# A fused attention and two-layer feed-forward kernel: the second pair's first scores get PSUM of their own, and two loads and two chunks of work change place

## The chip, the core and the metric

The kernel runs on one core of a Trainium2 chip. The core has five engines with an instruction queue each: TensorE (PE in the profile; its weight loads are PEld), VectorE (DVE), ScalarE (ACT), GpSimd (POOL) and SyncE (SP, which here only issues DMAs). Each queue runs in the order in which the program was written, and engines wait for each other through semaphores. TensorE writes its results into PSUM, 128 partitions of 8 banks; a bank holds 512 fp32 numbers a partition. The metric is the device time of one execution in microseconds (us), as the median of several runs.

## What is computed

With 2 batches, 12 heads, 448 positions and a head size of 64 (cut from the reference):

```
scores = q @ k.T / 8, upper triangle masked with -1e9
attn   = exp(scores - max) ; attn /= sum + 1e-9
x      = (attn @ v) as 896 tokens x 768
xn     = x / sqrt(mean(x*x) + 1e-6) * rms_g
y      = (silu(xn @ w_gate) * (xn @ w_val)) @ w_out      # 768 -> 1536 -> 768
out    = relu(y @ w_in)**2 @ w_out2                      # 768 -> 2048 -> 768
```

All of it is fp32.

## The kernel before

**Pairs.** Attention runs over 12 pairs of heads (two heads of one batch, side by side on the 128 partitions); function `step(p)` writes one pair. Its steps, by the short names used from here on:

- *s1* (lines 362 and 366): masked scores of query rows 0 to 127 (128 keys) and 256 to 383 (384 keys), in two chunks of 128 and 384 columns a head, into one PSUM buffer of 1024 numbers (two banks). *s2* (lines 362 to 378): those of rows 128 to 255 (256 keys) and 384 to 447 (448 keys), into another buffer of that kind.
- maxima on VectorE (lines 408 and 406), their negative on ScalarE (line 413, tile `nb`), exponentials with sums on ScalarE (line 433; four for s1 into `p1`, three for s2 into `p2t`).
- reciprocals of the sums on VectorE (lines 448 and 449; *r1* for s1, *r2* for s2), and the seven scalings by them on GpSimd (line 459).
- *tp* and *tp2*: transposes on TensorE (line 475), two PSUM tiles `t` of one bank for `p1` and two for `p2t`; each is copied to SBUF (`pt`, line 311) by ScalarE or VectorE.
- *o*: probabilities times values on TensorE (lines 508 and 513), one bank; then a copy into a `row` tile, its square (line 538 or 540), and the sum of squares (line 543).

After six pairs the first batch can be normalised (function `norm`, lines 575 to 613), and the first products of the feed-forward part can begin (function `whole_tiles`, matmuls of line 897, into the score buffers). When all pairs are done the second batch is normalised, and the remaining 2097 matmul instructions (line 693) run to the end. Weights are loaded in chunks (`raw`, line 633), unpacked on ScalarE (lines 646 and 641) and VectorE (line 651), and split into a high and a low part (`ring`, lines 268, 270 and 678).

**PSUM.** Two score buffers `s` (four banks), three `t` banks, one `o` bank. With two score buffers, a pair's s1 takes the buffer that held the s1 of the pair before it; it can start when that pair's four exponentials are done.

**Order.** The steps are not written out in their final order. `step` and the others give each step a due time, the engines that may run it with a cost on each, and the steps and buffers that it needs (`add`); `Order.run` is a planner that goes through a modelled time and issues what can go first, choosing an engine where there is a choice. So a change of a buffer or of a due time moves instructions on all engines, and from one engine to another.

**The start.** Twelve matmuls on zeros (`WARM`, line 1065) run while the first loads are under way; `IDLE = (5, 3)` puts five more behind pair 0's s2 and three behind pair 1's s1, into the `o` bank. They compute nothing.

Of the kernel before, what the change touches and what calls it, by code (L numbers as in the profile page):

```python
# [9 lines left out]
F32 = mybir.dt.float32  # L10
# [4 lines left out]
AF = mybir.ActivationFunctionType  # L15
ALU = mybir.AluOpType
PSUM = bass.MemoryType.PSUM

B, H, S, D = 2, 12, 448, 64
DM, DF1, DF2 = 768, 1536, 2048  # L20
P = 128
# [3 lines left out]
NF1 = DF1 // P  # L25
NF2 = DF2 // P
NPAIR = H // 2
WARM = 12
IDLE = (5, 3)
ACC = 0.0  # L30
CN = 112
# [1 line left out]
STRIDE = 5.5  # L33
# [22 lines left out]
class Order:  # L56
# [15 lines left out]
    def add(self, due, opts, f, after=(), new=(), uses=(), mode=None, begin=0.0, prev=(), port=False):  # L72

        t = dict(due=due, opts=opts, f=f, port=port, after=[a for a in after if a], new=list(new), uses=list(uses) + list(new),
                 mode=mode, begin=begin, end=None, eng=None, i=len(self.tasks), prev=[a for a in prev if a])
        for b in t["uses"]:
            b.left += 1
        self.tasks.append(t)  # L80
        return t
# [106 lines left out]
def tile_attention_moe_moe2(ctx: ExitStack, tc: tile.TileContext, qk, v, wg, wv, wo, w2i, w2o, rms_g, out):  # L188
# [12 lines left out]
    nc = tc.nc  # L201
# [5 lines left out]
    psum = ctx.enter_context(tc.tile_pool(name="psum", bufs=1, space=PSUM))  # L207
# [8 lines left out]
                  s=([P, 1024], F32))  # L216
    order = Order(dict(qk=3, v=3, p1=2, p2=2, pt=2))
    add, chain, buf = order.add, order.chain, order.buf
# [3 lines left out]
    def have(pool, **n):  # L222
        for name, k in n.items():
            for _ in range(k):
# [9 lines left out]

                order.more(name, make)

    def banks(name, *which):
        for i in which:
            order.more(name, lambda i=i: psum.tile([P, 512], F32, tag=f"b{i}", name=name, bufs=1))

    have(psum, s=2)
    banks("t", 0, 1, 2)
    banks("o", 3)
    have(pw, raw=2, wt=2, st=4, ring=8)
    have(pt_, snap=5, tt=2, uu=2, part=6, row=14)

# [3 lines left out]
    warm = atc.tile([P, 256], BF16, name="warm")  # L250
# [5 lines left out]
    g_sb = const.tile([P, NCC], F32, name="g_sb")  # L256
# [6 lines left out]
    def E(c):  # L263
        return {"A": nc.scalar, "D": nc.vector, "P": nc.gpsimd}[c]
# [13 lines left out]
    NPR = B * NPAIR  # L278
# [4 lines left out]
    for i, fill in enumerate((1.0, -1.0e9 * float(D) ** 0.5)):  # L283
        for k in range(2):
            for sl in (slice(0, D), slice(D, P)):
                t = half[sl, 2 * i + k]
                nc.gpsimd.affine_select(
                    out=t, in_=t, pattern=[[-1, P]], compare_op=ALU.is_ge if i else ALU.not_equal, fill=fill,
# [6 lines left out]
    for i in range(NV):  # L295
        t = atc.tile([P, 4, 2 * D], F32, name=f"vt{i}")
# [3 lines left out]
    for i in range(2):  # L300
        t = atc.tile([P, 2, 512], F32, name=f"p2t{i}")
# [11 lines left out]
    def A_(n, acc=0):  # L313
        return 0.17 + 0.00085 * n + (0.08 + ACC if acc else 0.0)
# [4 lines left out]
    def P_(n, two=False):  # L319
        return 0.2 + 0.0022 * n if two else 0.22 + 0.0009 * n  # L320
# [10 lines left out]
    def step(p):  # L331

        z = pairs[p]
        T0 = p * STRIDE
        bq, bv, b1, b2, bp1, bp2 = (order.buf(n) for n in ("qk", "v", "s", "s", "p1", "p2"))
        bpt, bo, bx = (order.buf(n) for n in ("pt", "o", "row"))

        def load_qk(e):
# [46 lines left out]


        if p < len(IDLE):
            bi = order.buf("o")

            def zeros(e):  # L390
                for _ in range(IDLE[p]):
                    nc.tensor.matmul(bi.tile[:, :256], warm[:, :P], warm, start=True, stop=True)

            add(T0, {"E": 0.11 * IDLE[p] + 0.16}, zeros, [(t3, t2)[p]], new=[bi], mode="w")
# [42 lines left out]
        ex_ = []  # L437
        for k, (buf, h, o, n, dst) in enumerate((
                ("s1", 0, 0, 128, "p1"), ("s1", 1, 0, 128, "p1"), ("s1", 0, P, 384, "p1"), ("s1", 1, P, 384, "p1"),
                ("s2", 0, 0, 256, "p2"), ("s2", 1, 0, 256, "p2"), ("s2", 0, 256, 448, "p2"))):  # L440
            b, bp = (b1, bp1) if k < 4 else (b2, bp2)
# [4 lines left out]
        def over(a, b):  # L446
            def f(e):
                nc.vector.tensor_scalar(z["r"][:, a:b], z["su"][:, a:b], 1.0e-9, 1.0, ALU.add, ALU.mult)
                nc.vector.reciprocal(z["r"][:, a:b], z["r"][:, a:b])  # L449
            return f  # L450

        r1 = add(T0 + 4, {"D": 0.37}, over(0, 4), ex_[:4], port=True)
        r2 = add(T0 + 7, {"D": 0.37}, over(4, 7), ex_[4:], port=True)

        def ml(k):
            def f(e):
                t = (z["p1"][:, k % 2, 0:128] if k < 2 else z["p1"][:, k % 2, 128:512] if k < 4 else
                     z["p2"][:, 0, (k - 4) * 256:(k - 3) * 256] if k < 6 else z["p2"][:, 1, :S])
                E(e).tensor_scalar(t, t, z["r"][:, k:k + 1], 1.0, ALU.mult, ALU.mult)  # L459
            return f  # L460

        ml_ = []
        for k, n in enumerate((128, 128, 384, 384, 256, 256, 448)):
            ml_.append(add(T0 + (5 if k < 4 else 8), {"P": P_(n)}, ml(k), [r1 if k < 4 else r2],
                           uses=[bp1 if k < 4 else bp2]))


# [57 lines left out]
        b = p // NPAIR  # L525
# [382 lines left out]
        have(p, part=18, row=18)  # L908

    add(0.0, {"X": 0.0}, rows_come, used)  # L910
    norm(0, (NPAIR + 4.5) * STRIDE, 5.0)
    norm(1, 0.0, 0.3)
    ws = []
    for k in range(2 * NE):
        due = 20 + 14.0 * k
        c, t = weights((wg, wv)[k % 2][k // 2], NCC, due, due, "wt")
        ws.append([form((c, o, t), 3, due) for o in (0, 3 * P)])
    whole_tiles(0, ws, 1000.0)
# [139 lines left out]
        f = halved(h2, k, highs(f), m, 2.0)  # L1058
        due = seven(w2o, k, f, of, due, k == 12, m=m)

    add(30.0, {"S": 2.0}, lambda e: nc.sync.dma_start(out=g_sb, in_=rms_g))
    with tc.manual_schedule():
        ps = psum.tile([P, 512], F32, tag="b3", name="warm", bufs=1)
        for _ in range(WARM):
            nc.tensor.matmul(ps[:, :256], warm[:, :P], warm, start=True, stop=True)
        order.run()
# [36 lines left out]
```

## Time and profile before

| | |
|---|---|
| median of 3 runs | 544.83 us (542.96 to 547.33) |
| the profiled execution | 543.9 us, its span 542.1 us |
| TensorE busy | 531.3 us, 98% of the span |
| VectorE, ScalarE, GpSimd busy | 447.8, 407.2, 311.3 us |
| granted TensorE clock | 1.00 through the span |

The span is the time from the first to the last instruction on the profiled core; 1.8 us of the execution's time lie around it. A busy time is the union of an engine's instructions. An arrow in brackets behind a row, as `[1.40 <-ACT p L433]`, is idle time of that engine just before the row, and what ended it. A row with `xN` merges N instructions that follow closely; its start is that of the first.

### The profile page before, as it was taken

How to read it: one execution, taken by the hardware profiler on the slowest of the kernel's cores; microseconds unless marked ns; L12 is line 12 of the kernel's file. 1: busy time of each engine (PE TensorE's matmuls, PEld its weight loads, DVE VectorE, ACT ScalarE, POOL GpSimd, SP SyncE). 2: the span in 40 equal slices, each digit the busy share in tenths (PEclk: the TensorE clock that was granted, in tenths of full speed). 3: DMA queues.
4: the chain of work that ended last, by engine and by line, in shares of the span. 5: the costliest groups of instructions: out<-in, count | busy, mean ns of one | idle time of the engine just before them, and what ended most of it. 6: DMA issues, size and time to landing. Idle time of an engine off the chain costs nothing.

```text
span 542.1 us, 8954 instructions
## 1 busy us (share of the span) xinstructions
PE 531.3 (98%) x3049; PEld 470.5 (87%) x3049; DVE 447.8 (83%) x831; ACT 407.2 (75%) x879; POOL 311.3 (57%) x349
## 2 busy tenths in 40 slices
PE   7999999999999999999999999999999999999997
PEld 5776766898899999999999989999898998899996
DVE  4788868599998887989867877998776799889795
ACT  4989887566867766679888777877878998886730
POOL 4666566215341452258999789242822886789910
PEclk9999999999999999999999999999999999999999
DMA  8255522113153333333544153134333333332333
GB/s 244 88 162 161 161 49 103 50 68 117 60 172 119 118 116 118 121 120 109 180 129 149 66 177 116 60 116 176 117 117 117 117 117 116 118 117 79 85 138 137
DMA packets 19502, 65.07 MB, mean 120 GB/s; under 512 B 2048, under 2 KB 8960, under 8 KB 19456
## 3 DMA queue, kind: packets, MB, share of 16 engines
q1 hardware_dynamic: 19376, 64.27, 36.0%
q8 instruction: 24, 0.39, 0.3%
q10 hardware_dynamic: 80, 0.23, 0.2%
q14 instruction: 22, 0.18, 0.1%
HBM read 61.74 MB, written 2.75 MB: 119 GB/s over the span
## 4 chain that ended last, share of the span: by engine, by line
PE 60%; DVE 18%; ACT 11%; DMA 4%; POOL 4%; issue 4%; DVEq 0%; POOLq 0%; ACTq 0%
PE m L693 45%; DVE ring L678 4%; DVE part L561 4%; PE t L475 4%; PE o L513 3%; PE s L362 3%; DMA raw<-in_w2i 2%; ACT ring L270 2%; PE s L375 2%; POOL part L561 2%; ACT s L641 2%; ACT raw L646 2%; PE s L897 1%; DVE s L651 1%; DVE row L725 1%
## 5 line engine op out<-in xcount | busy, mean ns | idle before, releaser
L693 PE MATMUL m<-part,ring 128*128 128x448 f32 x2097 | 424.4, 364 | 2.8 <-ACT snap L311 1.4
L693 PEld LDWEIGHTS m<-part,ring 128*128 128x128 f32 x2097 | 392.6, 188 | 34.4 <-ACT snap L311 4.4
L561 POOL TENSOR_TENSOR part<-row,part 128x448 fp32r<-128x448 f32 x103 | 122.5, 1210 | 51.1 <-ACT part L270 50.2
L678 DVE TENSOR_TENSOR ring<-s,ring 128x384 fp32r<-128x384 f32 (+1 forms) x159 | 83.1, 537 | 28.7 <-ACT ring L270 28.0
L725 POOL TENSOR_TENSOR row<-row 128x448 f32<-128x448 f32 x64 | 76.7, 1214 | 29.8 <-ACT row L1040 12.0
L270 ACT CAST ring<-s 128x384 fp32r<-128x384 f32 (+1 forms) x159 | 72.1, 470 | 25.7 <-PE m L693 12.9
L270 ACT CAST part<-row 128x448 fp32r<-128x448 f32 x133 | 70.1, 572 | 7.4 <-POOL wt L705 3.3
L646 ACT ACTIVATE raw<-raw 128x768 uint32<-128x768 uint8 (+1 forms) x70 | 62.7, 897 | 10.6 <-DMA raw<-in_w2i 3.7
L641 ACT ACTIVATE s<-raw 128x768 f32<-128x768 f32 (+1 forms) x64 | 53.6, 849 | 9.4 <-DVE ring L678 8.0
L651 DVE SCALAR_TENSOR_TENSOR s<-s,raw 128x768 uint32<-128x768 uint32 (+1 forms) x64 | 48.0, 749 | 6.4 <-ACT s L641 5.4
L268 POOL TENSOR_SCALAR ring<-st 128x384 fp32r<-128x384 f32 (+1 forms) x12 | 6.2, 512 | 79.1 <-DVE st L705 68.2
L270 ACT CAST ring<-st 128x384 fp32r<-128x384 f32 (+1 forms) x52 | 24.7, 504 | 25.3 <-DVE st L705 21.9
L678 POOL TENSOR_TENSOR ring<-st,ring 128x384 fp32r<-128x384 f32 (+1 forms) x39 | 38.0, 989 | 6.7 <-ACT ring L270 5.9
L705 DVE TENSOR_TENSOR s<-s,st 128x384 f32<-128x384 f32 (+1 forms) x62 | 34.2, 551 | 1.7
L561 DVE TENSOR_TENSOR part<-row,part 128x448 fp32r<-128x448 f32 x43 | 32.0, 769 | 2.8 <-ACT part L270 2.6
L408 DVE TENSOR_REDUCE mx<-s 128x2 f32<-128x256 f32 (+2 forms) x36 | 24.0, 687 | 11.2 <-PE s L378 6.3
L705 DVE TENSOR_TENSOR st<-st,s 128x384 f32<-128x384 f32 (+1 forms) x62 | 32.9, 531 | 0.2
L459 POOL TENSOR_SCALAR p<-p,r 128x128 f32<-128x128 f32 (+1 forms) x48 | 23.0, 497 | 16.7 <-DVE r L449 16.2
L311 ACT COPY snap<-m 128x448 f32<-128x448 f32 x51 | 27.1, 531 | 3.8 <-PE m L693 3.8
L459 POOL TENSOR_SCALAR p2t<-p2t,r 128x256 f32<-128x256 f32 (+1 forms) x36 | 22.7, 644 | 9.2 <-DVE r L449 5.3
L362 PE MATMUL s<-qk 64*128 64x128 f32 (+2 forms) x144 | 24.7, 426 | 2.0 <-ACT p L433 1.4
L979 DVE TENSOR_TENSOR row<-m,row 128x448 f32<-128x448 f32 x36 | 22.1, 618 | 3.8 <-PE m L693 3.5
(100 smaller groups left out, 574.3 us busy)
## 6 DMA issues: line engine op xcount, KB each, us to landing
raw<-in_w2i SPq DMA_DIRECT2D x16, 768.0 KB, 4.2
raw<-in_wg SPq DMA_DIRECT2D x12, 768.0 KB, 4.7
raw<-in_wv SPq DMA_DIRECT2D x12, 768.0 KB, 4.3
raw<-in_wo SPq DMA_DIRECT2D x12, 768.0 KB, 4.3
raw<-in_w2o SPq DMA_DIRECT2D x12, 768.0 KB, 4.6
qk<-in_qk SPq DMA_DIRECT2D x11, 448.0 KB, 3.8
raw<-in_w2o SPq DMA_DIRECT2D x6, 512.0 KB, 3.8
out_t<-row SPq DMA_DIRECT2D x12, 224.0 KB, 1.9
```

What stands on the lines that cost most here:

```text
L270: eng.copy(o, i)
L311: (nc.scalar.copy if e == "A" else nc.vector.tensor_copy)(o, i)
L362: nc.tensor.matmul(s[:, h, o:o + n], z["qk"][BOTH[h], 0, qs], z["qk"][BOTH[h], 1, :n], start=True, stop=False)
L459: E(e).tensor_scalar(t, t, z["r"][:, k:k + 1], 1.0, ALU.mult, ALU.mult)
L561: E(e).tensor_sub(bs.tile[:, 1], bf.tile, bs.tile[:, 0].bitcast(F32))
L641: nc.scalar.activation(bt.tile[:, :n * P], br.tile[:, :n * P, 1].bitcast(F32), AF.Prelu, scale=2.0 ** -112, alpha=2.0 ** 32)
L646: nc.scalar.activation(br.tile[:, :n * P, 0], b, AF.Copy, scale=1.0 / 32, bias=-31.0 / 64)
L651: nc.vector.scalar_tensor_tensor(dst.tile[:, :b - a].bitcast(U32) if dst else u, u, 3, br.tile[:, a:b, 0], ALU.logical_shift_left, ALU.bit ...
L678: E(e).tensor_sub(br.tile[:, 1, :n], num(), br.tile[:, 0, :n].bitcast(F32))
L693: nc.tensor.matmul(bank.tile[:, :S], bw.tile[:, a, i], x[:, c], start=first and i == 0 and k == 0, stop=last and i == n - 1 and k == 2, sk ...
L705: (E(e).tensor_add if plus else E(e).tensor_sub)(bs.tile[:, o:o + m * P], x, y)
L725: E(e).tensor_sub(bs.tile, a[0].tile, b[0].tile)
```

## The change

Line numbers in the rows of the changed program are those of the changed file. The edits, one by one:

1. A pool `psum0` with one score buffer `s0` is opened beside `psum`; it occupies two banks that were the third `t` bank and the `o` bank. Pair 1's s1 is written into it. A step without an engine, `banks_come`, closes the pool once pair 1's four exponentials are issued, opens a pool `psum1` in its place and hands out the third `t` bank and the `o` bank.
2. The zero matmuls behind pair 0 and pair 1 go into a `t` bank, those at the very start into bank b0 and are 13 instead of 12.
3. The load of `rms_g` (3 KB) is due at -12 instead of 30; the first weight chunks are due at 24, 37, 50, 63 instead of 20, 34, 48, 62.
4. The normalisation of the first batch is due half a pair earlier, with its steps 6 instead of 5 apart.
5. The last three scalings of the last pair may also run on ScalarE.

```
-WARM = 12
+WARM = 13
...
+    first = ExitStack()
+    psum0 = first.enter_context(tc.tile_pool(name="psum0", bufs=1, space=PSUM))
+    more = dict.fromkeys(range(4), psum)
...
-            order.more(name, lambda i=i: psum.tile([P, 512], F32, tag=f"b{i}", name=name, bufs=1))
+            order.more(name, lambda i=i: more[i].tile([P, 512], F32, tag=f"b{i}", name=name, bufs=1))
+
+    def banks_come(e):
+        first.close()
+        more[2] = more[3] = ctx.enter_context(tc.tile_pool(name="psum1", bufs=1, space=PSUM))
+        banks("t", 2)
+        banks("o", 3)
...
-    banks("t", 0, 1, 2)
-    banks("o", 3)
+    order.more("s0", lambda: psum0.tile([P, 1024], F32, tag="s0", name="s0", bufs=1))
+    banks("t", 0, 1)
...
-        bq, bv, b1, b2, bp1, bp2 = (order.buf(n) for n in ("qk", "v", "s", "s", "p1", "p2"))
+        bq, bv, b1, b2, bp1, bp2 = (order.buf(n) for n in ("qk", "v", "s0" if p == 1 else "s", "s", "p1", "p2"))
...
-            bi = order.buf("o")
+            bi = order.buf("t")
...
+        if p == 1:
+            add(T0 + 2, {"X": 0.0}, banks_come, ex_[:4])
...
-                E(e).tensor_scalar(t, t, z["r"][:, k:k + 1], 1.0, ALU.mult, ALU.mult)
+                if e == "A":
+                    nc.scalar.activation(t, t, AF.Copy, scale=z["r"][:, k:k + 1])
+                else:
+                    E(e).tensor_scalar(t, t, z["r"][:, k:k + 1], 1.0, ALU.mult, ALU.mult)
...
-            ml_.append(add(T0 + (5 if k < 4 else 8), {"P": P_(n)}, ml(k), [r1 if k < 4 else r2],
+            ml_.append(add(T0 + (5 if k < 4 else 8), {"P": P_(n), **({"A": A_(n)} if p == NPR - 1 and k >= 4 else {})}, ml(k), [r1 if k < 4 else r2],
...
-    norm(0, (NPAIR + 4.5) * STRIDE, 5.0)
+    norm(0, (NPAIR + 4) * STRIDE, 6.0)
...
-        due = 20 + 14.0 * k
+        due = 24 + 13.0 * k
...
-    add(30.0, {"S": 2.0}, lambda e: nc.sync.dma_start(out=g_sb, in_=rms_g))
+    add(-12.0, {"S": 2.0}, lambda e: nc.sync.dma_start(out=g_sb, in_=rms_g))
...
-        ps = psum.tile([P, 512], F32, tag="b3", name="warm", bufs=1)
+        ps = psum.tile([P, 512], F32, tag="b0", name="warm", bufs=1)
```

TensorE before, from pair 1's s1 (`s_205`) to pair 2's s1 (`s_292`); masks and weight loads are left out:

```order
L362 MATMUL s_205<-qk_143 128x128 x2
...
L362 MATMUL s_205<-qk_143 128x384 x2
...
L392 MATMUL o_229<-warm_75 128x256
...
L475 MATMUL t_235<-ident_77,p1_188 128x128 x4
L475 MATMUL t_240<-ident_77,p1_188 128x128 x4
L362 MATMUL s_250<-qk_143 128x256 x2
...
L475 MATMUL t_274<-ident_77,p2t0_123 128x128 x4
L475 MATMUL t_283<-ident_77,p2t0_123 128x128 x4
L362 MATMUL s_292<-qk_147 128x128 x2
...
L362 MATMUL s_292<-qk_147 128x384 x2
```

The same stretch in the changed kernel (`s0_205` is pair 1's s1 in its own pool, `s_235` its s2, `s_278` pair 2's s1):

```order
L373 MATMUL s0_205<-qk_148 128x384 x2
...
L403 MATMUL t_228<-warm_78 128x256
...
L373 MATMUL s_235<-qk_148 128x256 x2
...
L491 MATMUL t_259<-ident_80,p1_192 128x128 x4
L491 MATMUL t_270<-ident_80,p1_192 128x128 x4
L373 MATMUL s_278<-qk_152 128x128 x2
...
L491 MATMUL t_291<-ident_80,p2t0_126 128x128 x4
L491 MATMUL t_305<-ident_80,p2t0_126 128x128 x4
L373 MATMUL s_278<-qk_152 128x384 x2
```

Pair 1's s2 has moved ahead of pair 0's tp, and the first chunk of pair 2's s1 ahead of pair 0's tp2. `t_291` lies in the bank that `banks_come` hands out.

VectorE in the changed kernel, behind the first maxima (`s_176` is pair 0's s2):

```order
L417 TENSOR_REDUCE mx_171<-s_176 128x1
L419 TENSOR_REDUCE mx_219<-s0_205 128x2
L459 TENSOR_SCALAR r_174<-su_173 128x4
L460 RECIPROCAL r_174<-r_174 128x4
L419 TENSOR_REDUCE mx_219<-s0_205 128x2
L459 TENSOR_SCALAR r_174<-su_173 128x3
L460 RECIPROCAL r_174<-r_174 128x3
```

Before, both of pair 1's maxima stood behind pair 0's r1; now the first stands ahead of it.

TensorE at the end of attention in the changed kernel, from pair 10's tp2 (`t_1344`) to pair 11's o (`o_1447`):

```order
L491 MATMUL t_1344<-ident_80,p2t0_126 128x128 x4
L491 MATMUL t_1355<-ident_80,p2t0_126 128x128 x4
L913 MATMUL s_1362<-part_1212,ring_576 128x448 x3
...
L491 MATMUL t_1374<-ident_80,p1_1309 128x128 x4
...
L524 MATMUL o_1388<-pt_1304,vt1_122 64x128 x2
...
L491 MATMUL t_1411<-ident_80,p2t1_128 128x128 x4
L491 MATMUL t_1418<-ident_80,p2t1_128 128x128 x4
L913 MATMUL s_1362<-part_1342,ring_576 128x448 x3
...
L524 MATMUL o_1447<-pt_1399,vt2_124 64x128 x2
```

Before, pair 10's o stood ahead of pair 11's tp, the two tiles of pair 11's tp2 stood apart with three product matmuls before each, and 18 product matmuls (line 897) came ahead of pair 11's o; now 15 do. The three scalings of pair 11's `p2t` are ScalarE instructions.

## Rows read from the trace of the kernel before

**Rows 1.** The page: span; busy us, share and count of each engine.

```profile
span 542.1 us, 8954 instructions
PE 531.3 (98%) x3049; PEld 470.5 (87%) x3049; DVE 447.8 (83%) x831; ACT 407.2 (75%) x879; POOL 311.3 (57%) x349
```

**Rows 2.** Busy us by stretch (A:B in us): PE, PEld, DVE, ACT, POOL, clock, DMA.

```profile
110.00:150.00 40.00, 39.59 (x196) 36.25 (x195) 39.90 (x72) 28.98 (x55) 13.86 (x12) 1.00 0.26 83
```

**Rows 3.** Timeline of TensorE at the start: start, us, engine, line, what.

```profile
4.11 0.68 PE L362 MATMUL s<-qk 64*128 64x128 f32 x2 [0.33 <-DMA qk<-in_qk]
...
7.86 0.72 PE L392 MATMUL o<-warm 128*128 128x256 bf16 x5
9.98 0.49 PE L362 MATMUL s<-qk 64*128 64x128 f32 x4 [1.40 <-ACT p L433]
...
10.39 0.90 PE L362 MATMUL s<-qk 64*128 64x384 f32 x4
...
17.10 0.44 PE L508 MATMUL o<-pt,vt 128*64 128x128 f32 x4
...
21.66 1.09 PE L475 MATMUL t<-ident,p2t 128*128 128x128 f32 x8
22.68 0.49 PE L362 MATMUL s<-qk 64*128 64x128 f32 x4
```

**Rows 4.** Timeline of ScalarE, VectorE and GpSimd at the start.

```profile
7.76 0.20 ACT L413 ACTIVATE nb<-mx 128x4 f32<-128x4 f32 x1 [4.93 <-DVE mx L408]
9.71 0.21 ACT L433 ACTIVATION_READ_ACCUMULATOR p<-s,nb 128x1 f32 x1
11.48 0.21 ACT L433 ACTIVATION_READ_ACCUMULATOR p2t<-s,nb 128x1 f32 x1
12.84 0.57 ACT L311 COPY pt<-t 128x512 f32<-128x512 f32 x1
11.41 1.29 DVE L408 TENSOR_REDUCE mx<-s 128x2 f32<-128x256 f32 x2 [1.07 <-PE s L366]
10.53 1.84 POOL L459 TENSOR_SCALAR p<-p,r 128x128 f32<-128x128 f32 x4 [5.40 <-DVE r L449]
13.15 1.54 POOL L459 TENSOR_SCALAR p2t<-p2t,r 128x256 f32<-128x256 f32 x3 [0.78 <-DVE r L449]
```

**Rows 5.** Timeline of the last pair: TensorE, then GpSimd.

```profile
94.25 0.44 PE L475 MATMUL t<-ident,p2t 128*128 128x128 f32 x2 [0.83 <-POOL p2t L459]
91.75 3.42 POOL L459 TENSOR_SCALAR p2t<-p2t,r 128x256 f32<-128x256 f32 x3 [0.43 <-DVE r L449]
```

**Rows 6.** Busy us, 22.68 to 87.70 us (nine stretches): their sum and mean.

```profile
sum 65.02, PE 64.47 PEld 46.01 DVE 52.54 ACT 56.29 POOL 42.14; mean PE 7.16 PEld 5.11 DVE 5.84 ACT 6.25 POOL 4.68
```

**Rows 7.** ScalarE by line, 22.68 to 87.70 us: busy us, mean ns, idle before.

```profile
L433 ACT ACTIVATE p2t<-s,nb 128x256 f32<-128x256 f32 (+1 forms) x27 | 14.1, 535 | 0.0
...
L413 ACT ACTIVATE nb<-mx 128x3 f32<-128x3 f32 (+1 forms) x18 | 3.8, 210 | 6.5 <-DVE mx L406 4.7 <-DVE mx L408 1.8
...
L538 ACT ACTIVATE tt<-row 128x448 f32<-128x448 f32 x5 | 3.0, 600 | 0.0
...
L270 ACT CAST ring<-wt 128x384 fp32r<-128x384 f32 x2 | 1.1, 544 | 0.0
L311 ACT COPY row<-o 128x448 f32<-128x448 f32 x2 | 1.1, 527 | 0.0
```

**Rows 8.** Timeline of SP's queue in the first 10 us: DMA issues.

```profile
0.72 1.19 SPq L341 DMA_DIRECT2D qk<-in_qk  x2
...
6.71 0.60 SPq L1061 DMA_DIRECT2D g_sb<-in_rms_g  x1
```

**Rows 9.** DMA issues in the same 10 us: KB each, median us to landing.

```profile
qk<-in_qk SPq DMA_DIRECT2D x3, 448.0 KB, 4.8
...
g_sb<-in_rms_g SPq DMA_DIRECT2D x1, 3.0 KB, 3.7
```

**Rows 10.** The page's costliest groups: busy us, mean ns of one, idle before.

```profile
L561 DVE TENSOR_TENSOR part<-row,part 128x448 fp32r<-128x448 f32 x43 | 32.0, 769 | 2.8 <-ACT part L270 2.6
```

## The prediction, made before the changed kernel ran

> **What bounds the kernel now.** I read the page first. TensorE is busy for 531.3 of 542.1 us [rows 1], so idle TensorE time is 10.8 us, and an edit that leaves TensorE's arithmetic alone (this one adds one matmul on zeros) can give back no more than what lies in those 10.8. The table of stretches then says who sits behind TensorE later: from 110 to 150 us VectorE is busy for 39.90 of 40 us and TensorE for 39.59 [rows 2], so there is no slack there for VectorE to take on work. The two places where the edits act are read from timelines: the start, where TensorE idles 1.40 us ahead of pair 1's s1, "ended by ACT p", which means by pair 0's exponentials [rows 3], and the last pair, where it idles 0.83 us for GpSimd's scalings of `p2t` [rows 5]. ScalarE between these places is read last, since the planner gives it more work there: busy 56.29 of 65.02 us [rows 6].
>
> A measurement of this kernel tells about 1%, 5.4 us, from no change. All that can be won at the two places is 2 to 3 us.
>
> **The start (edit 1, with the zeros of edit 2).** Before, pair 0's exponentials run from 7.76 to 9.92 us (the last row starts at 9.71 and takes 0.21), 2.16 us [rows 4], and pair 1's s1 waits for the buffer until 9.98. In the changed order it has a buffer, so it starts when the five zero matmuls end, at 7.86 + 0.72 = 8.58 [rows 3]. That doesn't make the rest 1.40 us earlier, because ScalarE is next in line. What it does, in order:
>
> - ScalarE finishes pair 0's last three exponentials at 11.48 + 0.21 = 11.69 as before [rows 4]. Pair 1's four come right behind if their maxima are there. VectorE begins both maxima at 11.41 before, when s1 is written, 1.43 us after s1's start, and takes 1.29 [rows 4]. Now s1 is written at about 8.58 + 1.43 = 10.0, and the maxima end at 11.3, or 11.7 with r1 of pair 0 between them. So pair 1's exponentials end at 11.69 + 2.16 = 13.85.
> - VectorE's queue: one of the two maxima stands ahead of pair 0's r1, and waits for pair 1's s1. So r1 slips, by less than 1.29 in any case and by some 0.3 as the smaller of the two maxima. Behind r1 wait GpSimd's scalings (1.84 from 10.53 [rows 4]), and behind them tp of pair 0; that is TensorE's idle time and not its path, since what follows waits longer:
> - the first tile of pair 0's tp2 lies in the bank that the pool hands out, so it waits for 13.85. The second one takes the bank of tp's first tile, whose copy (0.57 [rows 4]) ScalarE can only start behind those exponentials: 13.85 + 0.57 = 14.42. Its scalings are done 0.1 before that: GpSimd is free of `p` at 10.53 + 0.3 + 1.84 = 12.7 and needs 1.54 [rows 4], 14.2 to 14.3.
> - From 14.42 TensorE has work without a gap: this tile, half of the 1.02 from 21.66 to 22.68; the second chunk of pair 2's s1, 0.90; o of pair 0, tp of pair 1 and s2 of pair 2, 4.56 together (17.10 to 21.66); tp2 of pair 1, 1.02 [rows 3]. That is 0.51 + 0.90 + 4.56 + 1.02 = 6.99, and pair 3's s1 starts at 21.41, with two hand-overs of 0.06 (as from 9.92 to 9.98) at 21.5 instead of 22.68. **Gain: 1.2 us**, bounds 0 (the waits at 13.85 and 14.42 come later by as much) and 1.4 (the whole idle time).
>
> **The end of attention (edit 5).** GpSimd takes 3.42 us for the last three scalings, from 91.75 to 95.17, and TensorE idles 0.83 for it [rows 5]. On ScalarE no such row exists. The nearest is its exponential on the same tiles, 0.535 us [rows 7], three of which are 1.6 us: the tiles would be there at 93.4 instead of 95.2, ahead of the 94.25 at which TensorE waited. I take **0.8**, all of the idle time; the bounds are 0 (ScalarE comes late to them, as it has its copies of `pt` to do) and 0.83. The Trainium skill, ScalarE: Activation LUTs, section What ACT_TABLE_LOAD costs, gives an ACTIVATE 186 ns + 0.833 ns a column, 93 ns for a pointer operand and 93 ns of overlap between neighbours: by that an estimate of 1.4 us for the three, which would not change the sum; no row here shows that form.
>
> **The loads (edit 3) and the 13th zero matmul.** The 13th lies in the 0.33 us in which TensorE waits for pair 0's load [rows 3]; one of five that take 0.72 is 0.14. Nothing. The load of `rms_g` moves from 6.71 to second on SP, between the two loads that issue from 0.72 to 1.91, and its own issue takes 0.60 [rows 8]. So pair 1's `qk` lands by 1.32 + 0.60 + 4.8 = 6.7 [rows 8, 9], under the 8.58 at which it is now needed: nothing, while 1.9 us of cover last. The bound above: its 128 small pieces hold up the transfer of pair 0's scores that is under way, by as much as the 0.60. That load was 3.7 us on its way for 3 KB, against 4.8 for 448 KB [rows 9]: the row shows latency, not bandwidth, and I take 0. The Trainium skill, DMA: Bandwidth & Descriptors, section Specifications, wants at least 512 B a piece for the full rate and says that smaller ones cost a read and a write; here they are 24 B. By that rule the load takes engines from the first scores, and the sum would be up to 0.6 higher; the row neither shows nor excludes it. The weight chunks are due up to four modelled us later; in the pairs, where they are used, TensorE idles 65.02 - 64.47 = 0.55 us in all [rows 6], so I cost this at 0 as well.
>
> **ScalarE in pairs 2 to 11 (edits 1, 4).** The planner gives it five more casts of `ring` (0.544), four copies of `row` (0.527), four squares (0.600) and two copies of `pt` (0.57) [rows 4, 7]: 2.7 + 2.1 + 2.4 + 1.1 = 8.3 us. It idles 65.02 - 56.29 = 8.73 [rows 6]. So it fits, with 0.4 to spare, but 6.5 of the idle time stand right before `nb`, where it waits for maxima [rows 7], and a copy that fills such a wait and ends late delays the exponentials. TensorE was held by ScalarE hardly at all in that stretch, as its 0.55 idle us show. The price is 0 if everything fits, and 8.3 - (8.73 - 6.5) = 6.1 if none of the waits before `nb` takes any of it. I take **+0.4**, near the lower end, because the planner puts most of the extra ones behind exponentials; a gain is possible too, down to -0.5, since GpSimd and VectorE, from which this work comes, let TensorE idle 0.55.
>
> **Behind attention (edit 4).** VectorE has three more instructions of line 561 (0.769 each [rows 10], 2.3 us), and two fewer instructions than before over the whole program, so it gives up others elsewhere; against 39.90 of 40 [rows 2] even that could show. Its work there is moved between chunks rather than added, so 0, bounds -0.4 and +2.3.
>
> **Sum:** -1.2 - 0.8 + 0.4 = -1.6 against the profiled execution's 543.9, which is 542.3. That execution is 0.9 below the median of 544.83; on the median the same sum is 543.2. I forecast in between, **542.8 us**.
>
> **Rivals.**
>
> *B. The idle time goes elsewhere as well.* ScalarE and VectorE take the work off GpSimd (busy 42.14 of 65.02 in the pairs [rows 6]), so that TensorE's small waits for it go, and the second chunk of pair 2's s1 or other work fills the gap ahead of 13.85. For it: TensorE idles 10.8 in all. Against: each further piece is under 0.6. All of 1.4 + 0.8 + 0.55 and 0.4 behind attention gives -3.1: 541 on the level above. Chance 0.15.
>
> *C. The gain at the start doesn't come.* A second wait takes the place of the first: the closed pool's bank binds `t_291` to pair 1's exponentials, and what hangs on it slips on: tp of pair 1, at 15.9 by the steps above, needs scalings that GpSimd can't begin before 14.3 and that take 1.84 [rows 4]. A slip of 1.2 along this chain puts pair 3's s1 at 22.68 again; or the small pieces of `rms_g` hold pair 0's scores by 0.6. Then -0.8 + 0.4 and up to +0.6: 543.9 (543.5 to 544.5 with the level). For it: ScalarE is the releaser of both waits. Chance 0.15.
>
> *D. ScalarE becomes the bound of pairs 2 to 11, and the kernel is slower.* It decides from where more than 2.2 us (8.73 less the 6.5 before `nb`) of the 8.3 can't be placed. If half of these waits can be filled, 8.3 - 2.2 - 3.3 = 2.8 us are left, and -2.0 + 2.8 = +0.8: 545.2 with the level; with none filled, +6.1 - 2.0: 548.5. For it: 56.29 + 8.3 is 99% of 65.02. Against: pairs end with TensorE idle 0.55 only, and waits for maxima are waits that a short copy fits into. Chance 0.23, of which 0.02 lies over 1% slower.
>
> **Numbers.** The forecast has 0.47 (541.7 to 544.3 by its own bounds), B 0.15, C 0.15, D 0.23. The range from 540.3 to 546.0 takes in B, C and the lower half of D. Faster by over 1% needs 5.4 us of 10.8 idle ones, 0.02; slower by over 1% only the far end of D, 0.03; the same 0.95.
>
> **What would show it.** Pair 1's s1 at 8.4 to 8.6 us with no wait for ACT in brackets; a wait of TensorE ahead of pair 0's tp2 that ends near 13.9, and one near 14.5; pair 3's s1 near 21.5; no wait for GpSimd at the last tp2, and ScalarE rows of about 0.5 for the scalings; ScalarE's idle time before `nb` below 6.5. If pair 3's s1 is near 22.7, C holds; if TensorE waits for ACT `pt` or `p` in pairs 4 to 10 for over 1 us together, D. I'm wrong if the time leaves 540.3 to 546.0, above all if the stretch from 110 us on has grown or shrunk by over 1 us, for which no step here stands.

## The result, and the profile after

The changed kernel takes 547.79 us as the median of 8 runs (547.10 to 549.59), the kernel before 545.05 in 8 runs beside it (542.18 to 547.33): a ratio of 1.0059, 95% interval 1.0039 to 1.0080, or 2.1 to 4.4 us more. (The ratio is an estimate over all runs; the quotient of the two medians is 1.0050.) 542.8 was forecast, with 546.0 as the upper end, so it went the other way. The profiled execution took 549.59 us, the longest of the eight. Its page begins:

```profile
span 547.8 us, 8959 instructions
...
PE 534.5 (98%) x3050; PEld 472.6 (86%) x3050; DVE 444.4 (81%) x829; ACT 415.8 (76%) x898; POOL 299.5 (55%) x332
```

Against [rows 1] the span grew by 5.7 us: TensorE is busy for 3.2 us more, with only one matmul more, and idle for 2.5 us more. To see where, I cut each profile at three instructions of TensorE: pair 3's s1, the first matmul of line 709 (693 before; "M0"), and the 150th behind it ("M150"). The table holds the times between them in us, read from the timelines; "clock" is the time by which the matmuls of the start have reached their fast pace.

| kernel | clock | pair 3's s1 at | to M0 | to M150 | to the end |
|---|---|---|---|---|---|
| before | 5 | 22.68 | 88.79 | 30.65 | 400.0 |
| changed | 9.4 | 23.71 | 90.97 | 32.92 | 400.2 |
| e1, chunks planned from 94 | 9.5 | 23.77 | 90.94 | 31.94 | 399.2 |
| e2, o ahead of tp | 5 | 21.65 | 88.83 | 31.70 | 399.8 |
| e3, pool alone | 5 | 21.73 | 91.60 | 30.95 | 400.0 |
| e4, without edit 5 | 9.9 | 24.18 | 91.04 | 31.70 | 398.7 |
| e5, e2 and chunks from 99 | 9.3 | 23.66 | 88.93 | 30.95 | 399.9 |
| e6, e5 without edit 5 | 9.0 | 23.64 | 90.03 | 30.95 | 400.6 |
| e7, slower GpSimd in the plan | 9.6 | 24.10 | 90.08 | 30.83 | 401.0 |
| e8, before, 22 zeros | 4.2 | 22.84 | 88.87 | 30.85 | 399.6 |
| e9, e5, 22 zeros | 6.5 | 22.80 | 88.82 | 30.95 | 399.8 |
| e10, changed, 22 zeros | 5.3 | 22.25 | 90.94 | 32.98 | 398.5 |
| e11, before, 4 zeros | 9.5 | 23.66 | 88.78 | 30.64 | 399.9 |
| e12, e5, 4 zeros | over 11 | 24.54 | 88.84 | 30.94 | 398.5 |

The columns in the middle repeat to 0.2 us for one order of instructions, whatever the clock did at the start; the last one wanders by 1.8 us in one and the same order (400.2 and 398.5 for the changed kernel with 13 and 22 zeros), so nothing is read from it. The changed kernel loses 2.2 us up to M0 and 2.3 behind it, and at the start it depends on the clock. One place after the other:

**The start.** Timeline of TensorE in the changed kernel; pair 1's s1 has no wait ahead of it any more (before: [rows 3], 1.40 us), and still begins later than before, at 10.57 instead of 9.98:

```profile
8.63 1.32 PE L386 MATMUL s<-qk 64*64 64x224 f32 x8
...
10.57 0.49 PE L373 MATMUL s<-qk 64*128 64x128 f32 x4
...
23.71 0.49 PE L373 MATMUL s<-qk 64*128 64x128 f32 x4
```

From 5 to 7 us TensorE is busy throughout in both profiles, but gets through 24 matmuls before and 13 after (stretch, busy us and count of PE, PEld, DVE, ACT, POOL, clock, DMA); first the kernel before, then the changed one:

```profile
5.00:7.00 2.00, 1.99 (x24) 1.65 (x26) 0.56 (x2) 0.00 (x0) 0.13 (x2) 1.00 1.10 294
```

```profile
5.00:7.00 2.00, 2.00 (x13) 1.69 (x15) 0.00 (x0) 0.00 (x0) 0.13 (x2) 1.00 1.14 280
```

The column of the granted clock says 1.00 in both; the pace of the matmuls tells the two levels, 1.2 and 2.4 GHz, apart here. The same scores take twice as long until about 9.4 us in this run of the changed kernel, and until 5 in the profiled run before. It isn't in the order of the start: e2 has the same one, with the clock up at 5. It does add 2.06 us to this profile (23.71 against 21.65 in e2).

**The end of attention.** TensorE's waits from 20 to 110 us (in total, times, longest) in the changed kernel:

```profile
PE t L491 <- POOL p L475: 2.5, 4, 1.1
PE o L529 <- ACT pt L322: 0.4, 1, 0.4
PE t L491 <- POOL p2t L475: 0.3, 1, 0.3
```

Before, the one large wait there was 0.83 us for `p2t` [rows 5]. It is gone, and two of 1.02 and 1.10 for `p` have come, at tp of pairs 10 and 11:

```profile
85.61 0.66 PE L491 MATMUL t<-ident,p 128*128 128x128 f32 x4 [1.02 <-POOL p L475]
86.19 0.44 PE L524 MATMUL o<-pt,vt 128*64 128x128 f32 x4
...
93.75 1.21 PE L491 MATMUL t<-ident,p 128*128 128x128 f32 x8 [1.10 <-POOL p L475]
94.90 0.44 PE L524 MATMUL o<-pt,vt 128*64 128x128 f32 x4
```

o of the pair before stands right behind each waiting tp. It was free to go, but the queue runs in order. What tp waits for, read backwards through three timelines of the changed kernel: pair 10's exponentials end at 81.46 on ScalarE; VectorE's r1 comes 1.4 us later, since a maximum that waits for s2 stands ahead of it; then GpSimd scales for 2.66 us, where four such scalings took 1.84 at the start [rows 4]. The last fence shows that for both pairs.

```profile
81.18 0.28 ACT L444 ACTIVATION_READ_ACCUMULATOR p<-s,nb 128x1 f32 x1
...
94.93 1.46 ACT L473 ACTIVATE p2t<-p2t,r 128x256 f32<-128x256 f32 x3
```

```profile
82.28 0.69 DVE L419 TENSOR_REDUCE mx<-s 128x2 f32<-128x512 f32 x1 [1.02 <-PE s L389]
82.89 0.16 DVE L459 TENSOR_SCALAR r<-su 128x4 f32<-128x4 f32 x1
```

```profile
83.45 2.66 POOL L475 TENSOR_SCALAR p<-p,r 128x128 f32<-128x128 f32 x4 [1.42 <-ACT pt L322]
...
91.60 2.66 POOL L475 TENSOR_SCALAR p<-p,r 128x128 f32<-128x128 f32 x4 [2.62 <-ACT pt L322]
```

The extra time lies in the second of the four, which took 1.20 us where the first took 0.37. Beside it VectorE ran two instructions that read two SBUF tiles each:

```profile
83.69 0.61 DVE L559 TENSOR_TENSOR snap<-snap,tt 128x448 f32<-128x448 f32 x1
84.22 0.62 DVE L577 TENSOR_TENSOR part<-row,part 128x448 fp32r<-128x448 f32 x1
```

It is the same in pair 11. At 22.34 us of this profile, with VectorE on maxima and a copy from PSUM, the four took 1.84. So by an estimate 0.8 us of each wait is GpSimd's delay beside VectorE; no run here takes those two instructions away.

All of TensorE's idle time from pair 3's s1 to M0 rose from 1.46 us to 3.45: 1.02 and 1.10 came, 0.83 went, and the small waits of the pairs up to pair 9 rose from 0.47 (0.28 for a copy of `pt`, 0.19 for `p`) to 1.12 (0.37 for a copy of `pt`; 0.22, 0.20 and 0.33 for GpSimd).

**Behind attention.** TensorE in the changed kernel, from M0 on:

```profile
114.68 18.62 PE L709 MATMUL m<-part,ring 128*128 128x448 f32 x92
134.74 10.69 PE L709 MATMUL m<-part,ring 128*128 128x448 f32 x52 [1.44 <-DVE ring L694]
146.25 3.99 PE L709 MATMUL m<-part,ring 128*128 128x448 f32 x18 [0.81 <-DVE row L828]
```

VectorE is full again, and GpSimd has half of the work that it had [rows 2]:

```profile
110.00:150.00 40.00, 37.74 (x186) 34.56 (x185) 39.33 (x71) 27.01 (x54) 7.19 (x7) 1.00 0.27 85
```

VectorE unpacks the third pair of weight chunks (line 651 before, 667 after) ahead of M0 in the kernel before, 7.3 and 6.4 us, and behind it in the changed one, by 2.9 and 4.3:

```profile
104.22 0.95 DVE L651 SCALAR_TENSOR_TENSOR wt<-wt,raw 128x768 uint32<-128x768 uint32 x1
105.09 0.55 DVE L651 SCALAR_TENSOR_TENSOR st<-wt,raw 128x384 uint32<-128x384 uint32 x1
```

```profile
117.60 0.94 DVE L667 SCALAR_TENSOR_TENSOR wt<-wt,raw 128x768 uint32<-128x768 uint32 x1
119.00 0.54 DVE L667 SCALAR_TENSOR_TENSOR st<-wt,raw 128x384 uint32<-128x384 uint32 x1
```

From 100 to 110 us, when VectorE has time (busy 3.9 us against 7.1 before), nothing of it is done. The program gives these chunks an earliest time, `begin=100.0`, on the planner's clock. In the changed plan, as I read it, the second batch's normalisation is ready for VectorE before that, so it goes first; e1 and e5 move the number.

### The profile page after: what moved, and what is told of

Read it like the earlier page. It is cut to its first block, busy times and chain, and to the rows that moved or that the text cites. A ratio compares the mean times of both kernels' runs of the same rounds, so it can differ in the third digit from the quotient of the medians.

```text
span 547.8 us, 8959 instructions
## 1 busy us (share of the span) xinstructions
PE 534.5 (98%) x3050; PEld 472.6 (86%) x3050; DVE 444.4 (81%) x829; ACT 415.8 (76%) x898; POOL 299.5 (55%) x332
## 4 chain that ended last, share of the span: by engine, by line
PE 58%; DVE 18%; ACT 13%; DMA 5%; issue 3%; POOL 2%; DVEq 0%; POOLq 0%; ACTq 0%; SPq 0%
PE m L709 47%; DVE part L577 4%; DVE ring L694 4%; PE o L529 2%; PE t L491 2%; DMA raw<-in_w2o 2%; ACT ring L281 2%; PE s L373 2%; ACT raw L662 2%; ACT s L657 2%; POOL p L475 2%; DVE s L667 2%; ACT row L1055 1%; PE s L386 1%; PE s L913 1%
## 5 line engine op out<-in xcount | busy, mean ns | idle before, releaser
L577 POOL TENSOR_TENSOR part<-row,part 128x448 fp32r<-128x448 f32 x100 | 117.3, 1196 | 58.0 <-ACT part L281 57.1
L741 POOL TENSOR_TENSOR row<-row 128x448 f32<-128x448 f32 x65 | 78.8, 1228 | 37.8 <-DVE row L853 13.7
L694 POOL TENSOR_TENSOR ring<-st,ring 128x384 fp32r<-128x384 f32 (+1 forms) x36 | 35.3, 995 | 6.3 <-ACT ring L281 5.6
L475 POOL TENSOR_SCALAR p<-p,r 128x128 f32<-128x128 f32 (+1 forms) x48 | 25.2, 542 | 21.7 <-DVE r L460 15.7
L577 DVE TENSOR_TENSOR part<-row,part 128x448 fp32r<-128x448 f32 x46 | 34.7, 780 | 0.9 <-ACT part L281 0.9
L475 POOL TENSOR_SCALAR p2t<-p2t,r 128x256 f32<-128x256 f32 (+1 forms) x33 | 21.1, 655 | 14.9 <-DVE r L460 8.2
L373 PE MATMUL s<-qk 64*128 64x128 f32 (+2 forms) x144 | 26.5, 448 | 0.2
```

The lines of the kernel that those rows point to most:

```text
L373: nc.tensor.matmul(s[:, h, o:o + n], z["qk"][BOTH[h], 0, qs], z["qk"][BOTH[h], 1, :n], start=True, stop=False)
L577: E(e).tensor_sub(bs.tile[:, 1], bf.tile, bs.tile[:, 0].bitcast(F32))
L694: E(e).tensor_sub(br.tile[:, 1, :n], num(), br.tile[:, 0, :n].bitcast(F32))
L741: E(e).tensor_sub(bs.tile, a[0].tile, b[0].tile)
```

## The experiments

**e1: the third pair of chunks may begin earlier.**

```diff
-                   begin=100.0 if ft == NE else 0.0, ...
+                   begin=94.0 if ft == NE else 0.0, ...
```

> The changed kernel, with the earliest planned time of the third pair of weight chunks at 94 instead of 100; all TensorE work up to the end of attention keeps its order, and VectorE unpacks these chunks ahead of the second batch's normalisation instead of behind it. Theory (late unpacking costs the stretch from 110 to 150 us): TensorE's idle time there falls from 2.26 us to under 0.8, and the kernel gets 1.5 to 2 us shorter than the changed one, some 1.002 of before. Rival (VectorE is full there, since it got three more subtractions): the idle time stays near 2 us and only changes place, ratio 1.006 as for the changed kernel.

547.77 us in 6 runs, ratio 1.0066 (1.0041 to 1.0091): not faster than the changed kernel. In the profile the stretch to M150 is 31.94 us, 1.0 less, half of what was expected, and TensorE's idle time from 110 to 150 us 1.60. The unpacking did come early, 12.3 and 10.8 us ahead of M0, and the two waits of 1.44 and 0.81 are gone; a new one has come:

```profile
134.55 15.67 PE L709 MATMUL m<-part,ring 128*128 128x448 f32 x77 [1.60 <-ACT snap L322]
```

Ahead of it two instructions of VectorE that take 0.55 to 0.61 us elsewhere took 1.40 and 1.51, beside three on GpSimd, one of 1.16 and two that took 3.00 together (1.16 for one alone):

```profile
128.14 1.40 DVE L741 TENSOR_TENSOR row<-row 128x448 f32<-128x448 f32 x1
129.46 1.51 DVE L694 TENSOR_TENSOR ring<-wt,ring 128x384 fp32r<-128x384 f32 x1
```

```profile
127.89 1.16 POOL L577 TENSOR_TENSOR part<-row,part 128x448 fp32r<-128x448 f32 x1 [4.13 <-ACT part L281]
129.00 3.00 POOL L741 TENSOR_TENSOR row<-row 128x448 f32<-128x448 f32 x2
```

So each delays the other, and VectorE lost 1.7 us there. The Trainium skill, SBUF — State Buffer, section Terms, says that VectorE and GpSimd share a pair of ports that one of them holds for a whole instruction while the other is blocked; these rows agree with that, with 1.40 us for an instruction that starts 0.25 us behind one on GpSimd, and so do the 2.66 us for the scalings above. Late unpacking is thus one cause in this stretch, not all of it.

**e2: o ahead of tp in the last two pairs.**

```diff
+                          prev=[pairs[p - 1]["va"]] if k == 0 and p >= NPR - 2 else ()))
...
-        va = add(T0 + 13, {"E": 1.96}, values, ...
+        va = z["va"] = add(T0 + 13, {"E": 1.96}, values, ...
```

> The changed kernel, with tp of pairs 10 and 11 bound to come behind o of the pair before, as it did before the change; up to there TensorE's order is that of the changed kernel. Theory (tp ahead of o leaves GpSimd no time for the scalings): the waits of 1.02 and 1.10 us for GpSimd's p in the last two pairs go below 0.3 each, and the end of attention comes 1.5 to 2 us earlier. Rival (ScalarE is full in the pairs and its exponentials come late): TensorE's idle time between 80 and 100 us stays at about 2 us, ahead of other steps.

545.94 us in 12 runs, ratio 1.0012 (0.9990 to 1.0034): the same as before within the interval. The stretch from pair 3's s1 to M0 falls from 90.97 to 88.83 us, which is 2.14 of the loss of 2.18. TensorE:

```profile
82.43 0.44 PE L525 MATMUL o<-pt,vt 128*64 128x128 f32 x4
...
84.31 1.09 PE L491 MATMUL t<-ident,p 128*128 128x128 f32 x8
...
89.25 0.44 PE L525 MATMUL o<-pt,vt 128*64 128x128 f32 x4
...
91.69 1.09 PE L491 MATMUL t<-ident,p 128*128 128x128 f32 x8
```

No wait for `p` at either tp; one of 0.34 us for a copy of `pt` at the second o is all. Pair 10's four scalings take 2.66 us here too, but o now covers them. The rival falls with it: ScalarE's load hardly differs between the two, 63.47 of 67.46 us in the changed kernel, and then 63.03 of 66.35 here (nine stretches, from pair 3's s1 into the last pair):

```profile
sum 67.46, PE 65.11 PEld 45.74 DVE 50.73 ACT 63.47 POOL 40.86; mean PE 7.24 PEld 5.08 DVE 5.64 ACT 7.05 POOL 4.54
```

```profile
sum 66.35, PE 65.06 PEld 45.95 DVE 50.69 ACT 63.03 POOL 41.97; mean PE 7.23 PEld 5.11 DVE 5.63 ACT 7.00 POOL 4.66
```

Since the plan behind the edit moved too, VectorE unpacked the first of the two chunks ahead of M0, and the stretch to M150 fell to 31.70.

This profile has the fast clock from 5 us on, so it shows the start as it was forecast:

```profile
8.52 0.49 PE L373 MATMUL s<-qk 64*128 64x128 f32 x4
...
13.89 1.10 PE L491 MATMUL t<-ident,p2t 128*128 128x128 f32 x8
14.92 0.92 PE L373 MATMUL s<-qk 64*128 64x384 f32 x4
...
21.65 0.49 PE L373 MATMUL s<-qk 64*128 64x128 f32 x4
```

**e3: the pool alone.** Edits 3, 4 and 5 and the 13th zero matmul taken back.

```diff
-WARM = 13
+WARM = 12
-    norm(0, (NPAIR + 4) * STRIDE, 6.0)
+    norm(0, (NPAIR + 4.5) * STRIDE, 5.0)
-        due = 24 + 13.0 * k
+        due = 20 + 14.0 * k
...
```

> The kernel before with edit 1 and the bank of edit 2 alone (12 zero matmuls, loads, normalisation, due times and GpSimd's scalings as before). Theory (the pool gains at the start, and what is lost comes from the planner's new order behind it): pair 3's s1 starts 1.0 to 1.2 us earlier than before when TensorE's clock rises at the same moment, and 110 to 150 us shows TensorE idle under 0.8. Rival (the closed pool's bank eats the gain): pair 3's s1 is where it was, at an equal clock. If TensorE's clock rises at another moment in this run (5.0 us before, 9.4 us in the changed kernel's), the start moves by up to 2 us for that alone, with the same waits.

549.70 us in 6 runs, ratio 1.0081 (1.0050 to 1.0113). The start is 0.95 us ahead of before at the same clock, a little under the 1.0 expected, and the loss comes behind it: 91.60 us to M0, 2.8 more than before, with seven waits for GpSimd's `p` (2.1 in all) and one of 1.0 for a copy of `pt`. So edit 1, with its bank, brings a loss without the others. The stretch to M150 is nearly as before, with both chunks unpacked ahead of M0. This profile is of the fastest run of the six (546.02, early clock); the median is 3.7 us above it, and the profile doesn't show why.

**e4: GpSimd does all scalings.**

```diff
-  {"P": P_(n), **({"A": A_(n)} if p == NPR - 1 and k >= 4 else {})}
+  {"P": P_(n)}
```

> The changed kernel without edit 5: GpSimd alone scales the last pair's p2t. Theory (edit 5 saves the wait at the last tp2): TensorE waits 0.5 to 1 us for GpSimd's p2t in the last pair, and the two waits for p stay at about 1 us each; VectorE's unpacking comes a little earlier, so 110 to 150 us shows less than 2.26 us of idle time. Rival (the scalings on ScalarE are what delays the end): the end of attention is not later than in the changed kernel.

547.39 us in 12 runs, ratio 1.0053 (1.0031 to 1.0075). The waits of 1.03 and 1.10 for `p` stayed, and none for `p2t` came at the last tp2: behind a tp that is late, GpSimd has time. To M0 it is 91.04, 0.07 more than the changed kernel. Half of the theory failed: edit 5 is worth nothing in this order. The stretch to M150 is 31.70, as the theory had it.

**e5: both repairs.** e2, and `begin=99.0`.

> As the kernel with tp behind o in the last two pairs, and with the earliest planned time of the third pair of weight chunks at 99 instead of 100, so that VectorE unpacks both chunks ahead of the second batch's normalisation, as before the change. Theory (tp ahead of o cost 2.1 us, late unpacking the rest): from pair 3's s1 to the first matmul of line 693's kind 88.8 us as before, the 150 matmuls behind it 31.0 us (30.65 before, 32.9 in the changed kernel, 31.7 with tp behind o alone); at an equal clock 0.5 to 1 us under before, ratio 0.998. Rival (VectorE's longer list is what costs): the 150 matmuls take 31.7 us or more again and the ratio stays at 1.001.

545.28 us in 12 runs, ratio 1.0006 (0.9983 to 1.0028). By stages it came as the theory has it: 88.93 us to M0 and 30.95 to M150, with both chunks unpacked ahead of M0 and GpSimd busy for 16.45 us from 110 to 150. As a whole it did not: no gain is measured against before. In its profile the clock rose at 9.3 us, and pair 3's s1 came at 23.66; e11 and e12 test whether that is why.

**e6: e5 without edit 5.**

> The kernel of the run above without edit 5: GpSimd alone scales the last pair's p2t. Theory (edit 5 takes a wait of 0.5 to 0.8 us off the last tp2): TensorE waits that long for GpSimd's p2t, and the first matmul of line 693's kind comes 0.5 to 0.8 us later, counted from pair 3's s1. Rival (other work covers it): no difference over 0.2.

546.69 us in 12 runs, ratio 1.0034 (1.0013 to 1.0055). To M0 it takes 90.03, 1.10 more than e5, with the wait that edit 5 takes away:

```profile
96.82 0.66 PE L491 MATMUL t<-ident,p2t 128*128 128x128 f32 x4 [0.93 <-POOL p2t L475]
```

Edit 5 is worth its 0.8 and more once tp no longer stands ahead of o.

**e7: a planner that knows slower scalings.**

```diff
-  {"P": P_(n), **(
+  {"P": 1.25 * P_(n), **(
```

> The changed kernel, with the planner told that a scaling on GpSimd takes 1.25 times as long; nothing else is edited, but the order changes on all engines from the first pairs on, and o comes ahead of tp at the end. Theory (the order failed because the scalings take longer on the chip than in the plan): no wait for GpSimd's p over 0.5 us in the last two pairs, and pair 3's s1 to the first matmul of line 693's kind under 90 us (90.97 in the changed kernel). Rival (the planner's order is as good as any, and ScalarE is the bound): waits of 1 us stay, for other steps.

546.07 us in 12 runs, ratio 1.0016 (0.9999 to 1.0033). The planner put o first by itself, and the waits for `p` fell from 2.5 to 0.2 us. But 90.08 to M0 misses the expectation by a little: the waits went to copies of `pt` (1.1 in three) and exponentials (0.8). The order differs from the first pairs on, so the run doesn't single out the last two; mending the number in the plan alone does not give back the order of before.

**e8: before with 22 zero matmuls.** `WARM = 22`.

> The kernel before with 22 instead of 12 zero matmuls at the very start. Theory (what makes runs of one kernel differ by up to 4 us is whether TensorE's granted clock is at 2.4 GHz when pair 0's scores begin): pair 0's scores start at 5.1 to 5.8 us and run at the fast clock, and the times of the runs lie within 2.5 us of each other instead of 4 to 5; the fastest runs are about 1 us slower than the fastest of before. Rival (the spread has another source): a spread of 4 us as before, all shifted by 1 us.

545.24 us in 12 runs, ratio 1.0003 (0.9988 to 1.0017), all from 543.87 to 545.86. Before with 12 zeros had 542.91 to 547.90 in the 35 runs beside it. So the spread is 2.0 us instead of 5.0, as the theory has it, though in 12 runs against 35, and before with 12 zeros spread over only 3.4 in the 23 runs beside e11. The fastest runs went up by 1.0.

**e9 and e10: e5 and the changed kernel, with 22 zeros.**

> The kernel with o ahead of tp in the last two pairs and the third pair of chunks planned from 99, with 22 instead of 13 zero matmuls at the very start. Theory (the parts add up: 0.9 us at the start and nothing lost behind it, and 22 zeros keep the runs together): all runs within 2.5 us, median 0.6 to 1 us under before with 22 zeros, some 544.4 us, ratio 0.998 to 0.9995 of before. Rival (with one score buffer more the start gains nothing once the clock is high from the first scores on): median as before with 22 zeros, 545.2.

> The changed kernel with 22 instead of 13 zero matmuls at the very start, to see the loss without the clock's part in it. Theory (2.2 us from tp ahead of o, 2.2 from late unpacking, less 1.0 at the start): 3.0 to 3.6 us above before with 22 zeros, some 548.5 us, ratio 1.007, and in its profile pair 3's s1 near 21.8. Rival (part of the loss was that the changed kernel met the low clock more often): under 2.5 us above before with 22 zeros.

e9 took 544.55 us in 11 runs, ratio 1.0011 (0.9999 to 1.0024) to before with 12 zeros (543.71 here); e8 had 1.0003. All of e9's runs lie within 2.5 us, as the theory has it, where e5's spread over 5.5. The rest of the theory fails, and the rival holds as to the time: no gain. In the profiles the zeros end at different times, since some run slow and the rest fast: pair 0's scores begin at 5.06 in e8, 5.61 in e10 and 5.85 in e9, and in e9 the first of them still run slow. So a gain of 1 us at the start drowns in that. Counted from pair 0's first score, pair 3's s1 comes after 17.78 us in e8, 16.64 in e10 and 16.95 in e9: the rival's reason, that nothing is gained at a high clock, does not hold. e10 took 546.15 us in 6 runs, ratio 1.0040 (1.0025 to 1.0056). That is 0.0037 or 2.0 us above e8's ratio, on the rival's side of 2.5, though the two intervals of some 0.8 us to either side leave the theory's 3.0 possible. Its pair 3's s1 is at 22.25, not near 21.8, as its zeros ended late. Its stages are those of the changed kernel, 90.94 and 32.98, so the losses behind the start are the same; what the clock adds to them is not measured more closely than that.

**e11 and e12: before and e5, with 4 zeros,** so that pair 0's scores run slow.

> The kernel before with 4 instead of 12 zero matmuls at the very start, so that TensorE has done little when pair 0's scores begin and they run at the low clock (1.2 GHz). Theory (before, a late clock costs 0.9 to 1.2 us, since pair 1's s1 waits for exponentials that need only the first half of pair 0's scores; in the changed order it costs 2.0, since TensorE itself is the bound there): pair 3's s1 at 23.6 to 23.9 us instead of 22.68, if the clock has risen by 10 us. Rival (a late clock costs the same in both orders): 24.6 or later.

> The kernel with o ahead of tp in the last two pairs and the third pair of chunks planned from 99, with 4 instead of 13 zero matmuls at the very start. Theory: pair 3's s1 at 23.6 to 23.9 us, the same as before with 4 zeros within 0.3, so that the pool gains nothing when the clock rises late; times within 0.2% of before with 4 zeros. Rival (the gain of 1.0 us at the start is there at either clock): pair 3's s1 0.8 to 1.2 us ahead of before with 4 zeros.

Before with 4 zeros took 544.76 us in 12 runs (ratio 1.0008, 0.9993 to 1.0022), e5 with 4 zeros 545.04 (1.0010, 0.9998 to 1.0022): the same. TensorE in e11, and then in e12:

```profile
5.19 1.66 PE L362 MATMUL s<-qk 64*128 64x384 f32 x4
...
10.59 0.49 PE L362 MATMUL s<-qk 64*128 64x128 f32 x4
...
23.66 0.49 PE L362 MATMUL s<-qk 64*128 64x128 f32 x4
```

```profile
11.40 0.49 PE L373 MATMUL s<-qk 64*128 64x128 f32 x4
...
24.54 0.49 PE L373 MATMUL s<-qk 64*128 64x128 f32 x4
```

At the slow pace the four matmuls of 384 columns take 1.66 us instead of 0.90 [rows 3]. The order of before loses 0.98 us by that (23.66 against 22.68), the order with the pool 2.9 (against 21.65 in e2) with a clock that rose later still, behind pair 0's scores. e5 and the changed kernel, whose clock rose at 9.3 and 9.4, lost 2.0 and 2.1. So with a late clock nothing of the gain at the start is left: pair 3's s1 is at 23.66 in e11 and at 23.64 to 24.18 in the six late profiles with the pool and 13 zeros. e11 came as expected; the 23.6 to 23.9 expected for e12 was missed, on the side of a loss.

## Why the prediction was wrong

- **The start: right in its times, in part by luck, and under a condition that I didn't see.** In e2 the times are those worked out: s1 of pair 1 at 8.52 (8.58), tp2 of pair 0 at 13.89 (13.85), the second chunk of pair 2's s1 at 14.92 (14.93), pair 3's s1 at 21.65 (21.5), a gain of 1.03 (1.2). But the two waits for ScalarE on which those times rest don't show. Pair 1's exponentials end at 13.74 and the copy of tp's first tile at 14.22, each some 0.15 us before TensorE comes to the transposes that need them (13.89 and 14.36). TensorE's one wait behind pair 1's s1 is 0.20 us for GpSimd's `p`, until 12.19 and so ahead of pair 0's tp, and from there it has work without a gap. That this chain and the one through ScalarE end together is luck. (The 2.16 us taken for four exponentials include the negative maxima, as the row at 7.76 is theirs [rows 4]; pair 1's took the same with theirs, from 11.58 to 13.74 in e2.) And all durations were taken from one execution in which the clock rose at 5 us. Where it rises late, the old order hides half of the slower scores behind ScalarE's exponentials, for which only the first half of pair 0's scores is needed; the new order has taken that idle time away, and pays in full. Over the runs the gain is about nothing.
- **The end of attention: the wrong sign.** The step that failed is "I take 0.8, all of the idle time". The wait for `p2t` did go, and three scalings took 1.46 us on ScalarE (1.6 by the row I took, 1.4 by the estimate from the Trainium skill, ScalarE: Activation LUTs, section What ACT_TABLE_LOAD costs). I had the order in which pair 11's tp stands ahead of pair 10's o before me, and priced only the engine that edit 5 relieves. What tp waits for there, r1 on VectorE and 2.66 us on GpSimd, was never worked out as it was for the start. The rows of before had a sign of it: three scalings of `p2t` took 1.54 us at the start and 3.42 at the end [rows 4, 5]. Instead of a gain of 0.8, the stretch up to M0 lost 2.18 us, with the 0.8 already in it; e2 gives back 2.14.
- **ScalarE in the pairs: right in sign, not the loss.** Its busy time rose to 94% of those pairs, near the 99% I had worked out, and TensorE's waits for its copies rose from 0.28 to 0.37 us only. With the waits for GpSimd the small waits up to pair 9 rose by 0.65, against the 0.4 that I took. In e2, with ScalarE at 95%, pair 3's s1 to M0 is as long as before, but with edit 5's gain (1.10 in e6) in it. Rival D's mechanism, which was to decide a slower kernel, did not decide it.
- **Behind attention: at the end of the bounds.** The term was 0, with bounds -0.4 and +2.3; it measured +2.27, in the stretch for which I had said that no step stood. I had looked at which instructions VectorE gets more of, not at where its unpacking stands against the normalisation. e1, e2 and e5 show the place of the unpacking to count for some of it, and e5 gives back 1.97 of the 2.27. How much is the order and how much the blocking between VectorE and GpSimd stays open: e1 unpacked earliest of all and kept 1.3.
- **The loads: not settled.** With `rms_g` second on the queue and up to 13 zeros, pair 0's scores began about 1 us later than in the others in two of eight profiles (5.11 in e4, 4.97 in e5), as their lower half landed later; the upper half is waited for until about 5.0 in the others too, so little was lost by it, and two of eight don't tell the small pieces from chance. The 13th zero took 0.21 us, as the first zeros run slow, and not 0.14; it still ended ahead of that load.
- **The range.** Its upper end held ScalarE's bound alone, and the term of the end of attention had none above zero. Two losses came together, 4.45 us.

The stages up to M150 give 3.4 us for the changed kernel against before at an early clock (-1.03 + 2.18 + 2.27, the start as in e2) and 4.5 at a late one (23.71 - 23.66 instead of -1.03); 2.1 to 4.4 are measured. No version of mine is measurably faster than the kernel before.

## What to carry to other kernels

Where a planner sets the order, an edit in one place is a new order in all places: find the steps that now stand ahead of a step that was ready, and work out for each what it waits for, back over all engines, as for the edit itself. Waits that a step is queued behind cost more than the engine loads tell; ScalarE at 94% cost little here, and each tp ahead of an o cost 1 us. Take idle time out of a stretch only after asking what it was absorbing in runs other than the profiled one.

## What the runs showed of the hardware

- With 12 or 13 zero matmuls from 1.05 us on, TensorE's pace rose by 5 us in three of nine profiles and at 9 to 10 in six, though TensorE waited in between for 1.11 us at most (ahead of pair 0's scores, in e4); one of the seven with 13 zeros was early, both of those with 12, which is too few to blame the 13th or the load of `rms_g`. The Trainium skill, TensorE: Matmul & The Clock Gate, section What's actually happening, says that the low level is where the engine starts, that activity releases it, and that the moment varies from run to run; the profiles agree: by 5 us in e2, at 9.4 in the changed kernel, with the same instructions up to there. The column of the granted clock, 1.00 throughout, did not show it.
- An instruction of VectorE of 0.61 us took 1.40 beside one on GpSimd. Four scalings on GpSimd took 1.84 us while VectorE ran maxima and copies from PSUM, and 2.66 where it ran two instructions with two SBUF tiles as input: a scaling of 0.37 us took 1.20 then.
